# A linear-attention and swish-MoE kernel: how the first two batches load k and v and lead into their first units

## The chip, the cores and the metric

The kernel runs on one core of a Trainium2 chip. Its time is the device time of one execution in microseconds (us); five runs are shown. One more view is the profile of one execution: what each engine did and when. The engines are named as in the profile: PE (TensorE matmul), PEld (its weight loads), DVE (VectorE), ACT (ScalarE), POOL (GpSimd), SP (SyncE, which issues nearly all DMAs).

## The reference

Eight batches, eight heads, 576 tokens, head size 64. Attention is linear: q is normalised by a softmax over its 64 features, k by a softmax over the tokens, and a 64x64 matrix k^T v per head replaces the attention matrix. The result, with heads side by side, goes through two weight matrices with a gated activation between.

```python
q_s = exp(q - max(q));  q_s = q_s / sum(q_s, axis=-1)
k_s = exp(k - max(k));  k_s = k_s / sum(k_s, axis=2)
kv  = einsum('bhsd,bhse->bhde', k_s, v)
att = einsum('bhsd,bhde->bhse', q_s, kv)
x   = att.transpose(0, 2, 1, 3).reshape(4608, 512)
h   = x @ w_in                       # 512 x 2048
g   = h * (1 / (1 + exp(-beta * h)))
out = g @ w_out                      # 2048 x 512
```

## The kernel before

**Tiles.** Each batch gives one chunk of 512 tokens; the last 64 tokens of all eight batches form a ninth chunk. For a chunk, a *unit* is one of 16 column blocks of w_in: `unit_a` (L312) issues four matmuls (K steps, kt = 0 to 3, one per pair of heads) into a PSUM tile `h`, then a tanh on ACT (`th`, L323) and an (th+1)*h on DVE (`g`, L325). `b_mm` (L346) issues the next so many matmuls of the product with w_out, in the order of the list `bq`, each 128x512, into `acc`; at the last of a row block `store` casts to `o` and sends it out.

**Attention of one batch.** `load_q` and `load_kv` fetch 4 heads at a time. k and v have nine tokens per group and a group is spread over two partitions: even partitions take tokens 0 to 4, odd ones tokens 4 to 8, so the fifth token (number 4) is loaded twice. `v_first` (L241) multiplies the first slot by `even`, 1 on even partitions and 0 on odd, so that it counts once; `v_cast` (L250) casts the other four slots of one head to bf16 into `va`. `q_exp`, `q_sum` and `q_div` make the softmax of q, `q_t_pe` (L187) transposes it on PE and copies it out, `k_exp` the exponentials of k. `kv_half` (L258) does for two pairs of heads five matmuls each into one PSUM tile, a reciprocal `rk` and two multiplications into `kvp`. `x_pair` (L282) multiplies a pair's kvp by q^T and casts the result into `xT`, the input of the units.

**What sets the order.** Scheduling is manual: every engine executes in the order in which the code issues. Batch 0's attention stands before all units, with `dummy` matmuls on zeros between (L434 to L474). Batch 1's stands between the units of chunk 0 and those of chunk 1 (L522 to L552), with calls of `b_mm` between its parts: 28, then 8 and 8 around the transposes of q, then three times 4. For later batches the parts hang as hooks on the units of the batch before (L477 to L512). Loads take buffers from one pool `ld` of 13; all of them for the first three batches are issued at the start, on SP's queue: q, k, v of batch 0, w_in, w_out in pairs of blocks, q of batch 1, the rest of w_out, k and v of batch 1, all of batch 2. POOL casts the weights (`cast_w_in`, `cast_w_out`).

**PSUM.** Pools of banks: `psH` 3 (h, and two of chunk 0's acc), `psB` 2 (acc, and the dummies' target), `psX` 2 (x and transposes), `psK` 1 (kv).

Of the kernel before, what the change touches and what calls it, by code (L numbers as in the profile page):

```python
# [9 lines left out]
F32 = mybir.dt.float32  # L10
# [6 lines left out]
def kernel(  # L17
# [61 lines left out]
    def unit(name):  # L79
        return ldp.tile([P, U], F32, tag="ld", name=name)  # L80
# [6 lines left out]
    def load_q(b, hf):  # L87
        t = unit(f"q{b}_{hf}")[:, 0 : 4 * NT * D].rearrange("p (h n) -> p h n", h=4)
        ld["q", b, hf] = t
        nc.sync.dma_start(  # L90
            t,
            q[b, 4 * hf : 4 * hf + 4, 0:CH, :].rearrange("h (p t) d -> p h (t d)", t=NT),
        )
# [6 lines left out]
                t[i * R : (i + 1) * R], q[2 * m + i, :, CH:S, :].rearrange("h s d -> s h d")  # L100
            )

    def load_kv(which, src, b, hf):
        t = unit(f"{which}{b}_{hf}").rearrange("p (h n) -> p h n", h=4)
        ld[which, b, hf] = t
        rows = src[b, 4 * hf : 4 * hf + 4, :, :].rearrange("h (r t) d -> r h (t d)", t=KT9)
        for i in range(2):
            n0 = i * (KT9 - K5) * D
            nc.sync.dma_start(t[i:P:2], rows[:, :, n0 : n0 + K5 * D])

    def load_w_in(n0, n1, k0=0, k1=KT):
        t = unit(f"wi{n0}_{k0}")[:, 0 : (k1 - k0) * (n1 - n0)].rearrange(
# [5 lines left out]
    def load_w_out(j0):  # L118
        t = unit(f"wo{j0}")[:, 0 : 2 * DM].rearrange("p (j n) -> p j n", j=2)
        nc.sync.dma_start(t, w_out_dram[:, j0 : j0 + 2, :])  # L120
        ld["wo", j0] = t
# [4 lines left out]
    def cast(eng, dst, src):  # L126
        if eng is nc.scalar:
            nc.scalar.copy(dst, src)  # L128
        elif eng is nc.gpsimd:
            if len(src.shape) > 3:  # L130
                for i in range(src.shape[1]):
                    cast(eng, dst[:, i], src[:, i])
                return
            n = 1
            for d in src.shape[1:]:
                n *= d
            nc.gpsimd.affine_select(  # L137
                out=dst, in_=src, pattern=[[0, n]], base=0, channel_multiplier=0,
                compare_op=ALU.is_equal, fill=fill0,
            )  # L140
        else:
            eng.tensor_copy(dst, src)  # L142
# [6 lines left out]
    def cast_w_out(j0, eng):  # L149
        cast(eng, w_out_b[:, j0 : j0 + 2, :], ld["wo", j0])  # L150
# [87 lines left out]
            ACTF.Exp,  # L238
        )

    def v_first(b, hf):  # L241
        nc.vector.tensor_scalar(  # L242
            va[b % 2][:, 0, 2 * hf : 2 * hf + 2, 0 : 2 * D].rearrange(
                "p j (two d) -> p j two d", two=2
            ),
            ld["v", b, hf][:, :, 0:D].rearrange("p (j two) d -> p j two d", two=2),
            even[:, 0:1], None, op0=ALU.mult,
        )

    def v_cast(b, h, eng):  # L250
        hf, a = divmod(h, 4)
        cast(
            eng,
            va[b % 2][:, 1:K5, h // 2, (h % 2) * D : (h % 2 + 1) * D],
            ld["v", b, hf][:, a, D:].rearrange("p (t d) -> p t d", t=K5 - 1),
        )

    def kv_half(b, half):  # L258
        ps = psK.tile([P, 2, VW], F32, tag="kv", name=f"kv{b}_{half}")
        for jj in range(2):  # L260
            j = 2 * half + jj
            for t in range(K5):
                nc.tensor.matmul(  # L263
                    ps[:, jj, :],
                    Ek[b][:, t, 2 * j : 2 * j + 2, :].rearrange("p h d -> p (h d)"),
                    va[b % 2][:, t, j, :],
                    start=(t == 0), stop=(t == K5 - 1),
                )
        rk = atn.tile([P, 2], F32, tag="rk", name=f"rk{b}_{half}")
        nc.vector.reciprocal(rk[:], ps[:, :, 2 * D])  # L270
        for h in (0, 1):
            r = slice(h * D, (h + 1) * D)
            nc.vector.tensor_tensor(  # L273
                kvp[b][r, 2 * half : 2 * half + 2, h * D : (h + 1) * D],
                ps[r, :, h * D : (h + 1) * D],
                rk[r, :].unsqueeze(2).to_broadcast((D, 2, D)),
                ALU.mult,
            )

    xT: dict = {}  # L280

    def x_pair(b, j, eng):  # L282
        if b not in xT:
            xT[b] = atn.tile([P, KT, NT, P], BF16, tag="xT", name=f"xT{b}")
        ps = psX.tile([P, NT, P], F32, tag="x", name=f"x{b}_{j}")
        nc.tensor.matmul(  # L286
            ps[:], kvp[b][:, j, :], qT[b][:, :, j, :], start=True, stop=True
        )
        cast(eng, xT[b][:, j], ps[:])

    def x_tail(b, eng):
        ps = psX.tile([P, HP, R], F32, tag="x", name=f"xt{b}")
# [16 lines left out]

    gs: dict = {}  # L310

    def unit_a(n, i):  # L312
        h = psH.tile([P, CH], F32, tag="h", name=f"h{n}_{i}")
        for kt in range(KT):
            nc.tensor.matmul(  # L315
                h[:],
                w_in_b[:, kt, i * P : (i + 1) * P],
                rhs_a(n, kt),
                start=(kt == 0),
                stop=(kt == KT - 1),  # L320
            )
        th = thp.tile([P, CH], BF16, tag="th", name=f"th{n}_{i}")
        nc.scalar.activation(th[:], h[:], ACTF.Tanh, scale=beta_h[:, i : i + 1])  # L323
        g = gtp.tile([P, CH], BF16, tag="g", name=f"g{n}_{i}")
        nc.vector.scalar_tensor_tensor(  # L325
            out=g[:], in0=th[:], scalar=1.0, in1=h[:], op0=ALU.add, op1=ALU.mult
        )
        gs[n, i] = g
        done_a[0] = n * NJ + i
# [53 lines left out]
    for hf in range(2):  # L383
        load_q(0, hf)
    for hf in range(2):
        load_kv("k", k, 0, hf)
    for hf in range(2):
        load_kv("v", v, 0, hf)
    nc.scalar.activation(beta_h[:, 0:1], zero[:, 0:1], ACTF.Exp)
    nc.scalar.dma_start(beta_r[:], moe_beta.rearrange("(j p) -> j p", p=P))  # L390
    load_w_in(0, 256)
# [3 lines left out]
        load_w_in(n0, n0 + 512, 2, 4)  # L395
    for j0 in range(0, 12, 2):
        load_w_out(j0)
    for hf in range(2):
        load_q(1, hf)
    load_w_out(12)  # L400
    load_w_out(14)
    for hf in range(2):
        load_kv("k", k, 1, hf)
        load_kv("v", v, 1, hf)
    for hf in range(2):
        load_q(2, hf)
    for hf in range(2):
        load_kv("k", k, 2, hf)
        load_kv("v", v, 2, hf)

    make_identity(nc, ident[:])
    make_identity(nc, identf[:])
    nc.gpsimd.memset(evens[:], 0.0)
# [16 lines left out]
    def dummy(m, n=CH):  # L430
        for _ in range(m):
            nc.tensor.matmul(warm[:, 0:n], zero[:, 0:P], zero[:, 0:n], start=True, stop=True)  # L432

    dummy(20)  # L434
    q_exp(0, 0, 4)
    q_exp(0, 4, 8)
    q_sum(0, 0, 4)
# [2 lines left out]
    q_div(0, 0, NT, nc.vector, 4, 8)  # L440
    k_exp(0, 0, 4)
    k_exp(0, 4, 8)
    dummy(4)
    for hf in range(2):
        q_t_pe(0, hf, 0, 4, nc.vector)
    bt = psH.tile([P, NJ], F32, tag="h", name="bt")
    nc.tensor.transpose(bt[:], beta_r[:], identf[:])
    nc.vector.tensor_scalar(beta_h[:], bt[:], 0.5, None, op0=ALU.mult)
    def v_casts(b, hf):
        v_first(b, hf)  # L450
        v_cast(b, 4 * hf, nc.gpsimd)
        v_cast(b, 4 * hf + 1, nc.gpsimd)
        v_cast(b, 4 * hf + 2, nc.vector)
        v_cast(b, 4 * hf + 3, nc.scalar)

    v_casts(0, 0)
    dummy(3)
    kv_half(0, 0)
    v_casts(0, 1)
    dummy(4, P)  # L460
    x_pair(0, 0, nc.vector)
    x_pair(0, 1, nc.scalar)
    kv_half(0, 1)
    cast_w_in(0, 0, nc.gpsimd, 0, 128)
    dummy(4, P)
    x_pair(0, 2, nc.vector)
    x_pair(0, 3, nc.scalar)
    cast_w_in(0, 0, nc.gpsimd, 128, 256)
    cast_w_in(256, 0, nc.gpsimd)
    for n0 in (512, 1024, 1536):  # L470
        for k0 in (0, 2):
            cast_w_in(n0, k0, nc.gpsimd)
    for j0 in range(0, 12, 2):
        cast_w_out(j0, nc.gpsimd)  # L474


    hooks: dict = {}  # L477
# [36 lines left out]

    for n in range(NCH):
        for i in range(NJ):
            unit_a(n, i)
            for f in hooks.get((n, i), []):
                f()
            if n:  # L520
                b_mm(2 if n == 1 and i < 4 else 4)
        if n == 0:  # L522
            b_mm(28)
            q_exp(1, 0, 4)
            q_exp(1, 4, 8)
            q_sum(1, 0, 4)
            q_sum(1, 4, 8)
            q_div(1, 0, NT, nc.gpsimd, 0, 4)
            q_div(1, 0, NT, nc.vector, 4, 8)
            cast_w_out(12, nc.scalar)  # L530
            cast_w_out(14, nc.scalar)
            for hf in range(2):
                k_exp(1, 4 * hf, 4 * hf + 4)
            q_t_pe(1, 0, 0, 4, nc.vector)
            b_mm(8)
            q_t_pe(1, 1, 0, 4, nc.vector)
            b_mm(8)
            for hf in range(2):
                v_first(1, hf)
                v_cast(1, 4 * hf, nc.gpsimd)  # L540
                v_cast(1, 4 * hf + 1, nc.gpsimd)
                v_cast(1, 4 * hf + 2, nc.vector)
                v_cast(1, 4 * hf + 3, nc.vector)
            kv_half(1, 0)
            b_mm(4)
            x_pair(1, 0, nc.vector)
            x_pair(1, 1, nc.scalar)
            b_mm(4)
            kv_half(1, 1)
            b_mm(4)  # L550
            x_pair(1, 2, nc.vector)
            x_pair(1, 3, nc.scalar)  # L552
    b_mm(10000)


# [28 lines left out]
```

The softmax here doesn't subtract the row's maximum and nothing guards it: scores larger than these inputs give would overflow.

## Time and profile before

| what | value |
|---|---|
| median of 5 runs | 297.86 us (297.46 to 301.06) |
| time of the run that was profiled | 298.06 us |
| span of the profiled execution | 296.3 us, mean granted clock 0.985 |
| HBM read and written | 38.81 MB and 9.44 MB |
| DMA rate, 8 to 16 us / 18 to 30 us / 40 to 55 us | 355 to 367 / 376 to 390 / 355 to 362 GB/s |
| granted clock, 11.5 to 14.5 us and 42 to 45 us | 0.50 |
| one 128x512 matmul, start to start | about 0.216 us at full clock, 0.43 at half |

How to read it: a row of the timeline gives the start in us, the duration, the engine, the line and operation, output and input tiles with their shapes, and how many were merged; in brackets the idle time before it and what ended that. The chain of waits is followed back from the last instruction: each piece is either work, or the time until what released it. A stretch table gives the busy time of each engine in each stretch. PEclk is the granted TensorE clock, in tenths of full speed.

The main events of the first 65 us, from the timeline: k-v products of batch 0 from 12.61; its first unit from 17.63; w_out products of chunk 0 from 31.52 to 37.87; exponentials of batch 1's q from 35.93 and of its k from 42.03 and 45.65; its k-v products from 46.66 and 51.18; its x pairs from 49.88 and 52.80; its first unit from 53.25.

### The profile page before, as it was taken

What the parts mean: (1) busy time and instruction counts of PE and PEld (TensorE: products, weight loads), DVE (VectorE), ACT (ScalarE), POOL (GpSimd) and SP (SyncE); (2) the same over time, 40 slices, a digit from 0 to 9 for tenths busy, and PEclk for the clock granted to TensorE, in tenths of its full rate; (3) what the DMA queues carried; (4) which work ended last, traced back from release to release, by engine and by line L of the source; (5) the groups of instructions that cost most, each with busy time, mean ns of one, the idle gap of its engine ahead of it and who ended that gap; (6) DMA issues with size and microseconds to landing.
All of it is one profiled execution on the core that took longest, in us unless ns stands there. A gap on an engine that the chain in (4) does not pass through costs nothing.

```text
span 296.3 us, 4129 instructions
## 1 busy us (share of the span) xinstructions
PE 280.7 (95%) x1417; PEld 132.0 (45%) x1444; DVE 165.7 (56%) x307; ACT 168.3 (57%) x268; POOL 73.2 (25%) x121
## 2 busy tenths in 40 slices
PE   8689967999999999999999999999999999999994
PEld 3444434344445444544454444444444444444441
DVE  7868365695686557654665475548544443343300
ACT  4458453683785568646864586458654544454511
POOL 6476631171072006210621063105300000000000
PEclk9799989999999999999999999999999999999998
DMA  7999999719929952997199619931400101031111
GB/s 237 360 383 384 371 365 357 273 56 285 301 82 257 351 76 75 255 354 81 71 228 367 97 73 226 369 63 70 108 18 20 72 36 38 0 71 39 35 71 71
DMA packets 54902, 52.19 MB, mean 176 GB/s; under 512 B 21072, under 2 KB 46688, under 8 KB 54880
## 3 DMA queue, kind: packets, MB, share of 16 engines
q1 hardware_dynamic: 54848, 51.92, 58.4%
q8 instruction: 11, 0.18, 0.3%
q14 instruction: 11, 0.09, 0.1%
q10 hardware_dynamic: 32, 0.01, 0.0%
HBM read 38.81 MB, written 9.44 MB: 163 GB/s over the span
## 4 chain that ended last, share of the span: by engine, by line
PE 78%; DMA 14%; DVE 4%; ACT 1%; issue 1%; POOL 0%; SPq 0%; DVEq 0%; ACTq 0%; POOLq 0%
PE acc L354 38%; PE h L315 35%; DMA wo<-in_moe_w_out_dram 7%; DMA v<-in_v_dram 5%; PE kv L263 3%; PE x L286 2%; DMA q<-in_q_dram 2%; DVE g L325 1%; DVE kvp L273 1%; ACT th L323 1%; DVE xT L142 0%; DVE o L369 0%; DVE qz L173 0%; PE xt L295 0%; DVE va L242 0%
## 5 line engine op out<-in xcount | busy, mean ns | idle before, releaser
L325 DVE SCALAR_TENSOR_TENSOR g<-th,h 128x512 bf16<-128x512 bf16 x144 | 98.6, 685 | 100.9 <-ACT th L323 100.7
L323 ACT ACTIVATE th<-h,beta_h 128x512 bf16<-128x512 f32 x144 | 99.0, 687 | 92.4 <-PE h L315 88.2
L354 PE MATMUL acc<-w_out_b,g 128*128 128x512 bf16 x560 | 145.5, 382 | 0.8
L315 PE MATMUL h<-xT,w_in_b 128*128 128x512 bf16 x502 | 128.2, 379 | 1.1 <-DVE xT L142 0.3
L315 PEld LDWEIGHTS <-w_in_b 128*128 128x128 bf16 x576 | 56.4, 98 | 69.0 <-issue 1.5
L354 PEld LDWEIGHTS <-g 128*128 128x128 bf16 x576 | 55.5, 98 | 64.0 <-issue 2.5
L177 POOL TENSOR_TENSOR Eq<-Eq,qz 128x512 bf16<-128x512 bf16 (+1 forms) x26 | 28.9, 1113 | 97.9 <-DVE qz L174 70.7
L371 ACT ACTIVATE o<-acc 128x512 f32<-128x512 f32 x34 | 20.2, 595 | 9.3 <-PE acc L354 9.3
L235 ACT ACTIVATE Ek<-k 128x640 bf16<-128x640 f32 (+1 forms) x28 | 22.6, 807 | 4.8 <-DMA k<-in_k_dram 4.8
L173 DVE TENSOR_REDUCE qz<-Eq 128x8 f32<-128x512 bf16 (+1 forms) x28 | 21.2, 756 | 3.9 <-ACT Eq L165 3.9
L165 ACT ACTIVATE Eq<-q 128x512 bf16<-128x512 f32 (+1 forms) x28 | 19.3, 690 | 6.8 <-DMA q<-in_q_dram 6.8
L137 POOL TENSOR_SCALAR_AFFINE_SELECT va<-v 128x256 bf16<-128x256 f32 x56 | 20.6, 406 | 9.8 <-DMA v<-in_v_dram 9.8
L315 PE MATMUL h<-xTt,w_in_b 128*128 128x512 bf16 x63 | 16.4, 379 | 0.1
L286 PE MATMUL x<-qT,kvp 128*128 128x512 bf16 x32 | 11.5, 380 | 2.9 <-DVE kvp L273 2.8
L128 ACT CAST xT<-x 128x512 bf16<-128x512 f32 x16 | 9.3, 580 | 7.9 <-PE x L286 7.9
L263 PEld LDWEIGHTS <-Ek 128*128 128x128 bf16 x160 | 10.5, 100 | 6.2 <-issue 4.0
L263 PE MATMUL kv<-va,Ek 128*128 128x130 bf16 x160 | 12.3, 225 | 0.7 <-DVE kvp L273 0.7
L142 DVE CAST xT<-x 128x512 bf16<-128x512 f32 x16 | 11.0, 685 | 1.0 <-PE x L286 1.0
L432 PE MATMUL warm<-zero 128*128 128x512 bf16 (+1 forms) x35 | 9.3, 426 | 1.3 <-DVE zero L382 1.3
L273 DVE TENSOR_TENSOR kvp<-kv,rk 64x128 bf16<-64x128 f32 x32 | 9.2, 289 | 1.3 <-DVE rk L270 0.5
L219 POOL TENSOR_TENSOR Et<-Et,zt 128x512 bf16<-128x512 bf16 x4 | 4.2, 1042 | 22.4 <-ACT th L323 11.4
L137 POOL TENSOR_SCALAR_AFFINE_SELECT w_in_b<-wi 128x1024 bf16<-128x1024 f32 (+1 forms) x9 | 8.5, 945 | 4.3 <-DMA wi<-in_moe_w_in_dram 4.3
(40 smaller groups left out, 70.5 us busy)
## 6 DMA issues: line engine op xcount, KB each, us to landing
k<-in_k_dram SPq DMA_DIRECT2D x32, 320.0 KB, 6.2
v<-in_v_dram SPq DMA_DIRECT2D x32, 320.0 KB, 7.7
q<-in_q_dram SPq DMA_DIRECT2D x16, 512.0 KB, 5.0
out_dram<-o SPq DMA_DIRECT2D x32, 256.0 KB, 2.4
wi<-in_moe_w_in_dram SPq DMA_DIRECT2D x8, 512.0 KB, 9.2
wo<-in_moe_w_out_dram SPq DMA_DIRECT2D x8, 512.0 KB, 12.2
qt<-in_q_dram SPq DMA_DIRECT2D x8, 128.0 KB, 8.4
out_dram<-o SPq DMA_DIRECT2D x8, 128.0 KB, 2.3
```

The source lines that it names most:

```text
L137: nc.gpsimd.affine_select(out=dst, in_=src, pattern=[[0, n]], base=0, channel_multiplier=0, compare_op=ALU.is_equal, fill=fill0,)
L165: nc.scalar.activation(Eq[b][:, :, h0:h1, :].rearrange("p t h d -> p h t d"), ld["q", b, hf][:, a : a + h1 - h0, :].rearrange("p h (t d) - ...
L173: nc.vector.tensor_reduce(qz[b][:, :, h], Eq[b][:, :, h, :], axis=AX.X, op=ALU.add)
L177: eng.tensor_tensor(Eq[b][:, t0:t1, h0:h1], Eq[b][:, t0:t1, h0:h1], qz[b][:, t0:t1, h0:h1].unsqueeze(3).to_broadcast((P, t1 - t0, h1 - h0, ...
L235: nc.scalar.activation(Ek[b][:, :, h0:h1, :].rearrange("p t h d -> p h t d"), ld["k", b, hf][:, a : a + h1 - h0, :].rearrange("p h (t d) - ...
L263: nc.tensor.matmul(ps[:, jj, :], Ek[b][:, t, 2 * j : 2 * j + 2, :].rearrange("p h d -> p (h d)"), va[b % 2][:, t, j, :], start=(t == 0), s ...
L286: nc.tensor.matmul(ps[:], kvp[b][:, j, :], qT[b][:, :, j, :], start=True, stop=True)
L315: nc.tensor.matmul(h[:], w_in_b[:, kt, i * P : (i + 1) * P], rhs_a(n, kt), start=(kt == 0), stop=(kt == KT - 1),)
L323: nc.scalar.activation(th[:], h[:], ACTF.Tanh, scale=beta_h[:, i : i + 1])
L325: nc.vector.scalar_tensor_tensor(out=g[:], in0=th[:], scalar=1.0, in1=h[:], op0=ALU.add, op1=ALU.mult)
L354: nc.tensor.matmul(acc[n, st][:], gs[n, j][:, st * P : (st + 1) * P], w_out_b[:, j, :], start=(j == 0), stop=(j == NJ - 1),)
L371: nc.scalar.activation(o[:], acc[n, st][:], ACTF.Copy, scale=0.5)
```

## The change

In batches 0 and 1 only:

- The fifth token is loaded once: odd partitions take tokens 5 to 8, and their first slot is set to zero by a POOL memset of the tile's first slot (128 x 4 x 64) before the loads. The second v tile of each is loaded in two halves of two heads.
- Batch 1's k is loaded before its v. The loads of batches 1 and 2 are issued in the code after the second cast of w_out on POOL (their place on SP's queue stays).
- `kv_half` is split into `kv_mm` (products of one pair), and `kv_norm` (reciprocal and multiplications of one or two pairs). In `lead_in` pairs 0 and 1 are normalised together, with the lower half on ACT; pairs 2 and 3 one at a time.
- `x_pair` is split into `x_mm` and `x_out`; x of pairs 0 and 1 is cast on ACT, that of pairs 2 and 3 in halves on DVE and ACT. The casts of v are spread in another way over POOL, DVE and ACT.
- `unit_mm` issues a part of a unit's K steps. The first two units of chunk 0, and the first three of chunk 1, have their first three K steps issued right after the last x product; the fourth follows in its old place.
- Batch 0's dummies: 24 instead of 20 and then 4; 3 between the two transposes of q; 4 after them; 2, 3, 2 and 2 wide ones in `lead_in`, where 3 wide and 8 narrow ones stood. Batch 1's calls of `b_mm` in the lead-in keep their sum of 12.

```diff
-    def load_kv(which, src, b, hf):
-        t = unit(f"{which}{b}_{hf}").rearrange("p (h n) -> p h n", h=4)
-        ld[which, b, hf] = t
-        rows = src[b, 4 * hf : 4 * hf + 4, :, :].rearrange("h (r t) d -> r h (t d)", t=KT9)
-        for i in range(2):
-            n0 = i * (KT9 - K5) * D
-            nc.sync.dma_start(t[i:P:2], rows[:, :, n0 : n0 + K5 * D])
+    def load_kv(which, src, b, hf, once=False, h0=0, h1=4):
+        if (which, b, hf) not in ld:
+            t = unit(f"{which}{b}_{hf}").rearrange("p (h n) -> p h n", h=4)
+            ld[which, b, hf] = t
+            if once:
+                nc.gpsimd.memset(t[:, :, 0:D], 0.0)
+        t = ld[which, b, hf][:, h0:h1]
+        rows = src[b, 4 * hf + h0 : 4 * hf + h1, :, :].rearrange("h (r t) d -> r h (t d)", t=KT9)
+        nc.sync.dma_start(t[0:P:2], rows[:, :, 0 : K5 * D])
+        if once:
+            nc.sync.dma_start(t[1:P:2, :, D:], rows[:, :, K5 * D :])
+        else:
+            nc.sync.dma_start(t[1:P:2], rows[:, :, (KT9 - K5) * D :])
...
+    def kv_mm(b, j):
+        if j % 2 == 0:
+            pool, tag = (psB, "acc") if b == 0 and j else (psK, "kv")
+            kvs[b, j // 2] = pool.tile([P, 2, VW], F32, tag=tag, name=f"kv{b}_{j}")
+        for t in range(K5):
+            nc.tensor.matmul(
+                kvs[b, j // 2][:, j % 2, :],
...
+    def kv_norm(b, j, n, eng=None):
+
+        ps = kvs[b, j // 2][:, j % 2 : j % 2 + n, :]
+        rk = atn.tile([P, 2], F32, tag="rk", name=f"rk{b}_{j}")
+        nc.vector.reciprocal(rk[:, 0:n], ps[:, :, 2 * D])
         for h in (0, 1):
             r = slice(h * D, (h + 1) * D)
+            if h and eng is nc.scalar:
+                for m in range(n):
+                    nc.scalar.activation(
+                        kvp[b][r, j + m, h * D : (h + 1) * D], ps[r, m, h * D : (h + 1) * D],
+                        ACTF.Copy, scale=rk[r, m : m + 1],
+                    )
+                continue
...
+    def x_out(b, j, eng, t0=0, t1=NT):
+        cast(eng, xT[b][:, j, t0:t1], xps[b, j][:, t0:t1])
...
+    def unit_mm(n, i, k0, k1):
+        if k0 == 0:
+            hs[n, i] = psH.tile([P, CH], F32, tag="h", name=f"h{n}_{i}")
+        for kt in range(k0, k1):
...
-    dummy(20)
+    dummy(24)
...
-    dummy(4)
-    for hf in range(2):
-        q_t_pe(0, hf, 0, 4, nc.vector)
+    q_t_pe(0, 0, 0, 4, nc.vector)
+    dummy(3)
+    q_t_pe(0, 1, 0, 4, nc.vector)
...
+    dummy(4)
...
+    def lead_in(b, fill):
+        v_first(b, 0)
+        v_cast(b, 0, nc.gpsimd)
+        v_cast(b, 1, nc.gpsimd)
+        v_cast(b, 2, nc.scalar)
+        v_cast(b, 3, nc.scalar if b else nc.vector)
+        fill(0)
+        kv_mm(b, 0)
+        kv_mm(b, 1)
+        v_first(b, 1, 0, 1)
+        v_cast(b, 4, nc.gpsimd)
+        v_cast(b, 5, nc.scalar)
+        kv_norm(b, 0, 2, nc.scalar)
+        if b == 0:
+            kv_mm(b, 2)
+        fill(1)
+        x_mm(b, 0)
+        x_mm(b, 1)
+        v_first(b, 1, 1, 2)
+        v_cast(b, 6, nc.gpsimd)
+        v_cast(b, 7, nc.scalar)
+        if b:
+            fill(2)
+            kv_mm(b, 2)
+        kv_norm(b, 2, 1, nc.vector)
+        x_out(b, 0, nc.scalar)
+        x_out(b, 1, nc.scalar)
+        fill(3)
+        kv_mm(b, 3)
+        x_mm(b, 2)
+        kv_norm(b, 3, 1, nc.vector)
+        x_out(b, 2, nc.vector, 0, 2)
+        x_out(b, 2, nc.scalar, 2, 4)
+        if b == 0:
+            cast_w_in(0, 0, nc.gpsimd, 0, 128)
+            cast_w_in(0, 0, nc.gpsimd, 128, 256)
+        fill(4)
+        x_mm(b, 3)
+        x_out(b, 3, nc.vector, 0, 2)
+        x_out(b, 3, nc.scalar, 2, 4)
+        for i in range(2 + b):
+            unit_mm(b, i, 0, 3)
+
+    def loads_1():
...
+        for hf in range(2):
+            load_kv("k", k, 1, hf, True)
+        load_kv("v", v, 1, 0, True)
+        load_kv("v", v, 1, 1, True, 0, 2)
+        load_kv("v", v, 1, 1, True, 2, 4)
...
+    lead_in(0, lambda m: dummy((2, 3, 2, 2, 2)[m]))
...
     for j0 in range(0, 12, 2):
         cast_w_out(j0, nc.gpsimd)
+        if j0 == 2:
+            loads_1()
...
-            unit_a(n, i)
+            unit_a(n, i, 3 if n < 2 and i < 2 + n else 0)
...
+            lead_in(1, lambda m: b_mm((0, 4, 4, 4, 0)[m]))
```

In batch 0, `lead_in` skips the third fill. Before, batch 1 had this in its place:

```python
            for hf in range(2):
                v_first(1, hf)
                v_cast(1, 4 * hf, nc.gpsimd)
                v_cast(1, 4 * hf + 1, nc.gpsimd)
                v_cast(1, 4 * hf + 2, nc.vector)
                v_cast(1, 4 * hf + 3, nc.vector)
            kv_half(1, 0)
            b_mm(4)
            x_pair(1, 0, nc.vector)
            x_pair(1, 1, nc.scalar)
            b_mm(4)
            kv_half(1, 1)
            b_mm(4)
            x_pair(1, 2, nc.vector)
            x_pair(1, 3, nc.scalar)
```

## The prediction

> **What bounds the kernel now.** I read the page first: shares by engine, the 40 slices, the chain by engine.
>
> ```profile
> span 296.3 us, 4129 instructions
> ...
> PE 280.7 (95%) x1417; PEld 132.0 (45%) x1444; DVE 165.7 (56%) x307; ACT 168.3 (57%) x268; POOL 73.2 (25%) x121
> ...
> PEclk9799989999999999999999999999999999999998
> DMA  7999999719929952997199619931400101031111
> ...
> PE 78%; DMA 14%; DVE 4%; ACT 1%; issue 1%; POOL 0%; SPq 0%; DVEq 0%; ACTq 0%; POOLq 0%
> ```
>
> TensorE is the bound over the whole (95% busy), so what can be won is its idle and half-clock time. The DMA engines are full in slices 1 to 6 and the clock dips in slices 1 and 5: the losses lie before 57 us. From 80 to 280 us a table of stretches gives PE 39.7 to 39.8 of every 40 us: nothing to win there, and the change leaves batches 2 to 7 alone. Next the chain of waits in order of time, from 36 to 56 us:
>
> ```profile
> 31.10 9.03 DMA wo<-in_moe_w_out_dram
> ...
> 40.14 7.22 DMA v<-in_v_dram
> ...
> 47.46 0.57 DVE va L242
> 48.02 0.60 DVE va L142 x2
> 48.62 0.09 DVE rk L270
> ...
> 49.88 0.60 PE x L286 x2
> ...
> 52.81 0.69 DVE o L369
> 53.50 0.61 DVE xT L142
> ...
> 54.16 0.59 PE h L315 x2
> ```
>
> Batch 1's last v tile lands at 47.36; then VectorE casts it (1.2 us) ahead of the reciprocal of the first two pairs, whose products had been ready since 47.39. So 6.8 us pass from landing to the first steady unit at 54.16. The timeline shows the rest:
>
> ```profile
> 2.13 3.79 POOL L426 MEMSET kvp<- 128x512 bf16 x8
> 2.44 3.52 DVE L421 TENSOR_SCALAR va<-va,even 128x8 bf16<-128x8 bf16 x2
> ...
> 40.63 0.62 PE L194 MATMUL tp<-ident,Eq 128*128 128x128 bf16 x8 [2.76 <-POOL Eq L177]
> ...
> 54.78 0.69 ACT L323 ACTIVATE th<-h,beta_h 128x512 bf16<-128x512 f32 x1 [0.75 <-PE h L315]
> ...
> 62.49 1.02 PE L315 MATMUL h<-xT,w_in_b 128*128 128x512 bf16 x4 [0.19 <-DVE g L325]
> ```
>
> PE stands 2.76 us before 40.63, waiting for batch 1's q. So batch 0's lead-in has that slack. At 62.49 PE waits for a g: in stretches of 1 us from 57 to 66, DVE is 0.90 to 1.00 busy. Whatever comes earlier at 54 us must therefore pass through VectorE's queue (g1 at 56.80, then no gap), and that queue starts when ScalarE's th0 does, at 54.78.
>
> **The change, part by part.**
>
> Fewer bytes. The odd partitions' rows of k and v shrink from 1280 to 1024 B in batches 0 and 1: 4 tiles x 256 rows x 256 B = 262 KB a batch. By bytes at the 360 GB/s of that stage: 0.73 us. By packets (the count stays): 2048 B rows moved at about 388 GB/s, 1280 B rows at about 358, or 84.5 and 57.2 ns a packet on each of 16 engines, so 256 B are 9.1 ns; 64 packets an engine: 0.58 us. I take 0.58 a batch. Batch 1's q comes 0.58 earlier, its last v 1.16 (47.36 to 46.2). The order becomes k, k, v, v. From wo's end at 40.1 - 0.58 = 39.5 in tiles of 1.66 us (1.8 less 0.144): k 41.2 and 42.8, first v 44.5, the halves of the second 45.3 and 46.2. Splitting it adds two DMAs a batch on SP's queue; an issue there takes 0.60 us at least, so 1.2 us a batch, before k and q of batch 2. Issue to landing of v was 6.4 us or more, so SP is ahead and I cost it nothing; without that lead 1.2 us.
>
> Eight memsets on POOL. 128x256 f32 has no row; 128x64 f32 took 0.14, 128x128 bf16 0.20, 128x512 bf16 0.52: 0.31 each, 1.24 for four. At the start they precede everything on POOL, so the kvp memsets end at 7.16, not 5.92. The row above shows what that does: two 8-element operations of DVE took 3.4 to 3.5 us and ended at 5.96, with POOL. The Trainium skill, "SBUF — State Buffer", section "Who interferes with whom", says that a VectorE tensor_scalar in a two-port mode and GpSimd share a port pair and the loser blocks for a whole instruction. Read by that, DVE would lose one memset (at most 0.52) and the additions would cost nothing; in the trace it lost all eight. I follow the trace: q_sum and DVE behind it start 1.24 later. The four memsets of batch 1 stand on POOL after w_out's second cast (29.03 + 1.04); SP issued batch 1's first k at 31.73, so they are ready 1 us before, and w_out's casts behind them recover 0.3 us a tile.
>
> Batch 0's lead-in. DVE reached v_first at 11.94, now 13.2. Three wide dummies between the transposes (0.43 each, as the clock is 0.50 from 11.2) put the second transposes at 12.6 to 13.7, its copy to 14.4, v_first to 14.9, the DVE cast to 15.15. Six more dummies end at 15.6, k-v products of two pairs 16.35, reciprocal and normalisation 17.1, then with 7 dummies (0.216 each), two single normalisations and the x pairs, the units start at about 19.7. Before, they ran from 17.7 (31.52 less 64 x 0.216). So 2.0 us later, and 3.5 if the half clock lasts a second 3.4 us. PE then ends its 28 w_out products at 39.9 (or 41.4), where q's transposes are ready at 40.05: the slack is eaten, the loss is small.
>
> The clock in batch 1. It was 0.50 from 41.65 to 45.07. The skill's "TensorE: Matmul & The Clock Gate", section "Why this matters for your kernels", asks for idle gaps of no more than about 3 us; by it neither the 2.76 nor a shorter gap would cost anything. The trace has half clock after 2.76, and after 1.34 followed by transposes (11.2). So a gap may still cost; no gap (39.9 to 40.05) need not. From the first transposes to the k-v products took 6.03 us at the mixed clock; at full clock 0.62 + 1.73 + 0.62 + 1.73 = 4.7. Start S of the products: PE gives 44.8 to 46.1, data 45.35 (v at 44.5, two casts 0.8). I take 45.7; before 46.66.
>
> From S to th0: two products 0.73; reciprocal 0.2; ScalarE's two 64x64 pieces have no row (128x1 ACTIVATE 0.20, 128x256 cast 0.41: 0.27 each) to S+1.5, under four w_out products to 1.6; x0 and x1 2.05; four products 2.9; third pair 3.3 (its half-v and three casts landed long before); four products 4.1; last pair and x2 4.7. On DVE o_3's 0.69 stands ahead of the last reciprocal: 5.0, then 0.17 and two singles of 0.25 to 0.29: x3 at 5.8 to 6.0, nine products of units 0 to 2 by 8.0, hiding x3's half copies (0.4), last K step of unit 0, th0 at S+8.3 = 54.0. Before 54.78.
>
> What is late next: ScalarE and VectorE. th1 no longer waits for PE (th0 to g1 was 2.02, now 0.59 + 0.52 + 0.69 + 0.02 = 1.8): 0.2 more. g4 and the unit at 62.49 come 0.78 + 0.2 = 1.0 us earlier; from there PE is the bound in both. The two more products per unit done ahead gain nothing: they wait there. The other moves (casts from DVE to ACT, x0 and x1 both on ACT, 0.58 each) lie under the w_out products; uncovered 0.6.
>
> Sum: span 296.3 - 1.0 = 295.3. Its run's time was 298.06, 1.76 above span; that gives 297.06, and 0.2 less for the median of 297.86: 296.8.
>
> **The rivals.**
> 1. Larger gain: VectorE is not the limit after 54 us and all of PE's lead counts. PE's effective start was 53.73 (two products done before 54.16) and becomes S+6.05 = 51.4 with S at 45.35: 2.3 us, 295.5. For it: PE 0.81 to 1.00 busy there too. Against: DVE 1.00 in five of those stretches.
> 2. No change: o_3 and the single normalisations stretch the end of batch 1's lead-in by 0.8 us, th0 stays at 54.8: 297.8. For: every step is serial between PE and DVE, as the 1.62 us wait at 49.88. Against: the 1.2 us of v casts ahead of the reciprocal are gone.
> 3. Slower: the half clock. If the thinned work from 11 to 18 us keeps it at 0.50 and batch 0's products slip more than 4.1 us (S past 46.7 moves th0 past 54.98, break-even), each further us counts in full; a second half-clock stretch from 45.07 to 48.5 alone costs 1.7. Together +1.5 to 3.2: 299.4 to 301. For: the dips stand in the trace. Against: after both dips the clock came back in 3.4 us.
> That it doesn't do what it says is excluded: in the program's order the six and nine early K steps stand as described.
>
> **How the numbers follow.** Forecast 57% (gain 0.5 to 1.5), rival 1 13%, rival 2 17%, rival 3 13%. Range 295.2 to 299.2: rival 1 with 0.3 to spare, and the lighter part of rival 3. About 1% (3 us) is what a measurement of this kernel tells from no change: faster by that 7% (half of rival 1, if the lead is larger than worked out), slower 8%, within 85%.
>
> **What would show it.** Right: last v of batch 1 by 46.4; DVE's first 128x8 operations until about 7.2; PE's wait before q's transposes of batch 1 under 1 us; th0 at 53.6 to 54.4; a wait for g at about 61.5. Wrong: last v landing at 47 or later, th0 after 55, PEclk 0.5 after 46 us, or no wait for g near 62.

## The result, and the profile after

| | before | after |
|---|---|---|
| median | 297.89 us (297.36 to 301.06, 44 runs) | 296.31 us (295.98 to 297.43, 23 runs) |
| ratio of after to before, 95% interval | | 0.9932 [0.9915, 0.9949] |
| HBM read | 38.81 MB | 38.28 MB |

The median is 1.58 us (0.5%) lower: inside the 1% that the prediction called "same", at 296.3 us where it had said 296.8, and a little more than the 0.5 to 1.5 us of its forecast. The ratio in the table is that of the means, which lie 2.0 us (0.7%) apart, because 19 of the 44 runs of before took 298.77 us or more. The executions of after fall into two kinds: with the profiled one there are 24, of which 17 have a span of 294.3 to 294.8 us at a granted clock of 0.997 to 1.0, and seven a span of 295.3 to 296.2 (clock 0.994 in six, 0.999 in one). The first profile, of a run of 297.92 us, is the longest of the seven. So it is read here for its mechanisms, and a second profile of the same kernel, from the common kind, for the gain.

First the page of the profiled execution of after; the lines answer to those of before.

```profile
span 296.2 us, 4168 instructions
PE 282.0 (95%) x1421; PEld 131.9 (45%) x1449; DVE 162.5 (55%) x308; ACT 172.1 (58%) x281; POOL 75.3 (25%) x129
PEclk9999989999999999999999999999999999999999
DMA  7999999729929971995199618931500110031111
PE 80%; DMA 11%; DVE 3%; ACT 2%; issue 1%; POOL 1%; SPq 1%; ACTq 0%; POOLq 0%
```

PE is as busy as before. The dip of PEclk in slice 1 (7.4 to 14.8 us) is gone, that in slice 5 (37 to 44.4 us) stands as before. A table of stretches resolves it: a clock of 0.87 from 40 to 42 us, 0.50 from 42 to 44 and 0.78 from 44 to 46. The timeline of the same execution (start, duration, engine, line, operation, tiles, idle time before and what ended it), ordered by stage:

```profile
0.80 0.56 POOL L108 MEMSET k<- 128x256 f32 x2 [0.29 <-POOLq L627]
1.29 0.56 POOL L108 MEMSET v<- 128x256 f32 x2
...
3.42 3.53 DVE L448 TENSOR_SCALAR va<-va,even 128x8 bf16<-128x8 bf16 x2
5.81 1.22 DVE L179 TENSOR_REDUCE qz<-Eq 128x16 f32<-128x1024 bf16 x1
...
12.61 1.16 PE L271 MATMUL kv<-va,Ek 128*128 128x130 bf16 x15
16.86 2.95 PE L350 MATMUL h<-xT,w_in_b 128*128 128x512 bf16 x12
20.22 4.04 PE L350 MATMUL h<-xT,w_in_b 128*128 128x512 bf16 x17 [0.42 <-DVE g L364]
...
24.89 3.33 SPq L90 DMA_DIRECT2D q<-in_q_dram  x2
...
40.55 0.62 PE L200 MATMUL tp<-ident,Eq 128*128 128x128 bf16 x8 [2.76 <-POOL Eq L183]
46.58 0.73 PE L271 MATMUL kv<-va,Ek 128*128 128x130 bf16 x10
...
55.04 0.69 ACT L362 ACTIVATE th<-h,beta_h 128x512 bf16<-128x512 f32 x1 [1.52 <-PE h L350]
...
62.55 1.02 PE L350 MATMUL h<-xT,w_in_b 128*128 128x512 bf16 x4 [0.74 <-DVE g L364]
```

What the reader is to see: the four new memsets shift POOL's start by 0.99 us; the two tiny operations of DVE again last 3.5 us, but the reduction of q (L179) starts at 5.81, as it did before. Batch 0's units start at 16.86 (before: 17.63), but PE then waits, 0.42 us for a g among other things, and w_out products start at 31.44 (before: 31.52). The wait before batch 1's q is 2.76 us, to the digit that of before; k-v products start at 46.58, th0 at 55.04, and the wait for a g at 62.55 lies where it lay before (62.49). In this execution nothing is won.

The second profile, of a run of 296.25 us with span 294.5 and clock 1.00 throughout, shows the kernel as it runs in 17 of 24 executions:

```profile
23.91 3.33 SPq L90 DMA_DIRECT2D q<-in_q_dram  x2
...
34.88 1.06 ACT L171 ACTIVATE Eq<-q 128x1024 bf16<-128x1024 f32 x1 [2.76 <-DMA q<-in_q_dram]
...
39.58 0.62 PE L200 MATMUL tp<-ident,Eq 128*128 128x128 bf16 x8 [2.00 <-POOL Eq L183]
...
44.15 1.24 POOL L143 TENSOR_SCALAR_AFFINE_SELECT va<-v 128x256 bf16<-128x256 f32 x3 [4.62 <-DMA v<-in_v_dram]
...
44.95 0.67 PE L271 MATMUL kv<-va,Ek 128*128 128x130 bf16 x9 [0.79 <-POOL va L143]
46.60 0.61 PE L312 MATMUL x<-qT,kvp 128*128 128x512 bf16 x2
...
50.80 2.52 PE L350 MATMUL h<-xT,w_in_b 128*128 128x512 bf16 x9
...
53.35 0.69 ACT L362 ACTIVATE th<-h,beta_h 128x512 bf16<-128x512 f32 x1 [1.52 <-PE h L350]
...
60.87 1.02 PE L350 MATMUL h<-xT,w_in_b 128*128 128x512 bf16 x4 [0.74 <-DVE g L364]
```

Here SP issues batch 1's q 0.98 us sooner than in the first profile (23.91 against 24.89), everything behind it comes sooner by the same, the clock stays full, and PE has to wait 0.79 us at 44.95 for POOL's casts of the first v: the start of the k-v products (one of them ran ahead at 43.94) is bound by data. th0 comes at 53.35, 1.4 us before that of before (54.78), and the wait for a g ends 1.6 us sooner (60.87 against 62.49). The spans differ by 1.8 us.

### The profile page after: what moved, and what is told of

Its sections match the earlier page's. It is cut to its first block, busy times and chain, and to the rows that moved or that the text cites. A ratio compares the mean times of both kernels' runs of the same rounds, so it can differ in the third digit from the quotient of the medians.

```text
span 296.2 us, 4168 instructions
## 1 busy us (share of the span) xinstructions
PE 282.0 (95%) x1421; PEld 131.9 (45%) x1449; DVE 162.5 (55%) x308; ACT 172.1 (58%) x281; POOL 75.3 (25%) x129
## 3 DMA queue, kind: packets, MB, share of 16 engines
HBM read 38.28 MB, written 9.44 MB: 161 GB/s over the span
## 4 chain that ended last, share of the span: by engine, by line
PE 80%; DMA 11%; DVE 3%; ACT 2%; issue 1%; POOL 1%; SPq 1%; ACTq 0%; POOLq 0%
PE acc L393 39%; PE h L350 36%; DMA q<-in_q_dram 5%; DMA wi<-in_moe_w_in_dram 4%; PE kv L271 3%; PE x L312 2%; DMA v<-in_v_dram 2%; DVE g L364 1%; DVE qz L179 1%; ACT th L362 1%; POOL Eq L183 1%; ACT Eq L171 1%; PE tp L200 0%; DVE kvp L292 0%; SPq L121 0%
## 5 line engine op out<-in xcount | busy, mean ns | idle before, releaser
L179 DVE TENSOR_REDUCE qz<-Eq 128x8 f32<-128x512 bf16 (+1 forms) x28 | 21.2, 756 | 3.9 <-ACT Eq L171 3.9
L134 ACT CAST xT<-x 128x512 bf16<-128x512 f32 (+1 forms) x20 | 10.6, 540 | 2.4 <-DVE xT L148 2.2
L459 PE MATMUL warm<-zero 128*128 128x512 bf16 x39 | 10.7, 420 | 1.3 <-DVE zero L421 1.3
L148 DVE CAST xT<-x 128x512 bf16<-128x512 f32 (+1 forms) x16 | 9.9, 619 | 0.1
L292 DVE TENSOR_TENSOR kvp<-kv,rk 64x128 bf16<-64x128 f32 (+1 forms) x34 | 9.3, 273 | 0.9
```

Of the source, the lines that this page charges most:

```text
L179: nc.vector.tensor_reduce(qz[b][:, :, h], Eq[b][:, :, h, :], axis=AX.X, op=ALU.add)
```

## The experiments

The theory from the first profile of after: the gain is one of data (the first v lands sooner, and the first pairs need no other v), and a stretch of half clock decides in which executions it is had. The rivals: the clock alone (dummy products would do the same for the kernel before), the order alone (without fewer bytes), either batch's part alone. Runs of e and f stand against runs of before on one chip (median of before there 299.2 and 299.1), those of g on another (297.9); ratios are compared, not medians.

### Executions of before

Three more profiles of the kernel before, unchanged; f0 has 12 timed runs too.

> The kernel before, unchanged, for a second profile of it: its runs fall in two groups on one chip, 297.2 to 297.8 and 299.2 to 300.2, at mean clocks that do not tell the groups apart (0.994 is in both), and the changed kernel has no second group. If the second group comes from the half clock falling later in batch 1's lead-in (from 45 us on, behind v's landing), its profile has half clock between 45 and 53 us and q's transposes at 40.6 as before. If it comes from batch 0's lead-in (half clock through the k-v products until 18 us), chunk 0's w_out products end after 40.5 us and q's transposes come later. If from the DMA, v of batch 1 lands 2 us later at an unchanged clock.

> The kernel before, unchanged: another profile, wanted from a run above 299 us. With either lead-in changed alone no run was above 298.8, so the runs above 299 need both old lead-ins. If they are those in which batch 0's half clock lasts to 18 us and delays chunk 0, and a half clock again falls on batch 1's chain behind v, then chunk 0's w_out products end after 40 us and PEclk is 0.5 after 45 us. If the profile is of the lower group: half clock at 11 to 15 and at 41 to 45, th0 near 54.8.

> The same once more: the kernel before, for a profile of a run above 299 us; the same expectations.

Against the other runs of before, f0's gave 1.0006 [0.9981, 1.0031]; its profile (298.24 us) repeats the one shown ahead, with the first x product at 50.03. The runs of before are of two kinds: of the 44, 24 lie at 297.36 to 298.06 and 19 at 298.77 to 301.06, one between. g0 (297.80, span 296.1) and g1 (299.36, span 297.6) are one of each. PE's timeline of g0:

```profile
40.37 1.04 PE L194 MATMUL tp<-ident,Eq 128*128 128x128 bf16 x8 [3.08 <-POOL Eq L177]
41.63 2.48 PE L354 MATMUL acc<-w_out_b,g 128*128 128x512 bf16 x7 [0.22 <-DVE Eq L177]
46.12 0.73 PE L263 MATMUL kv<-va,Ek 128*128 128x130 bf16 x10
49.60 0.60 PE L286 MATMUL x<-qT,kvp 128*128 128x512 bf16 x2 [1.89 <-DVE kvp L273]
52.97 0.59 PE L315 MATMUL h<-xT,w_in_b 128*128 128x512 bf16 x2
```

and of g1, the same kernel:

```profile
40.40 0.62 PE L194 MATMUL tp<-ident,Eq 128*128 128x128 bf16 x8 [3.10 <-POOL Eq L177]
41.08 1.67 PE L354 MATMUL acc<-w_out_b,g 128*128 128x512 bf16 x7
44.76 0.73 PE L263 MATMUL kv<-va,Ek 128*128 128x130 bf16 x10
49.63 1.04 PE L286 MATMUL x<-qT,kvp 128*128 128x512 bf16 x2 [3.28 <-DVE kvp L273]
50.46 1.91 PE L354 MATMUL acc<-w_out_b,g 128*128 128x512 bf16 x4
54.54 0.59 PE L315 MATMUL h<-xT,w_in_b 128*128 128x512 bf16 x2
```

In g0 the half clock falls on the transposes and w_out products at 40 to 44 us (eight transposes 1.04 us, 0.62 at full clock). It costs nothing: the first x product waits for v all the same, and comes at 49.60. In g1 those products run at full clock, PE is through 1.36 us sooner, and then stands 3.28 us; x comes at 49.63, and now the half clock falls on the chain behind it (x 1.04 instead of 0.60, four w_out products 1.91 instead of 1.03), where each lost us counts: units at 54.54 instead of 52.97. The clock averaged over the span is 0.994 in both. So a mean clock doesn't tell what a stretch of half clock costs; its place does. v's landing was the same in both (POOL's last casts began at 47.21 and 47.24). No other run of the upper kind, up to 301.06, has a profile.

### The common execution of after

The kernel after, unchanged; its profile is the second one above.

> The kernel after, unchanged: a look at another execution, since the profiled one was one of the slower seven of its 24 runs. Theory: two things part the executions, when SP can issue batch 1's q (after the landing of w_in's seventh tile) and whether PE's clock stays full from 40 to 46 us. A run of the common group (span 294.3 to 294.8) then has q issued at 23.6 to 24.1, its exponential at 34.6 to 35.0, no half clock from 40 to 46, k-v products waiting for the first v's casts at 44 to 45, and th0 at 53.0 to 53.5. With only one of the two, the span is 295.0 to 295.6; with neither, 296.0 to 296.3. Rival: q's issue is noise that the later stages absorb. Then a run of the common group can have q at 35.5 or later.

The span of 294.5 came with q's issue at 23.91, q's exponential at 34.88, no half clock, th0 at 53.35: all inside the theory's numbers, and the rival (q at 35.5 or later) is out. What ties the issue of q to w_in is in the chain of waits of the first profile (start, duration, what):

```profile
13.64 11.18 DMA wi<-in_moe_w_in_dram
24.83 0.02 SPq L90
24.89 10.94 DMA q<-in_q_dram
```

SP's issue waits for a w_in tile to land, the eighth load before it on that queue. From q's issue everything follows at a fixed distance: the first v's cast on POOL began 20.20 us after it in the first profile and in e3, 20.22 to 20.25 in the second, e1 and f3. So the landing of w_in's seventh tile is what the bytes of batch 0 can move. With the new batch 0 q's issue came at 23.7 to 24.0 in four profiles, at 24.5 in f2's, and at 24.7 and 24.9 in two (mean 24.19). With the old one it came at 24.7 to 25.1 in five. In a sixth, e2's, it came at 24.04 (mean of the six 24.75), but there POOL's cast of the eighth tile began only at 26.02, as late as in the other five (26.05 to 26.48; 25.0 to 25.3 in the four early ones), and the last v was no sooner: POOL cast it from 47.11, against 47.21 in g0.

Late q and half clock came together in the first profile; e3's (below) has them apart. Its kernel differs only behind the last x product, its q was late (24.67) and its clock full, and its k-v products ran on from 45.67. Of the 1.63 us between the two starts, 46.58 and 44.95, q's issue therefore makes 0.98 and the half clock the other 0.65.

### One part undone

Batch 0 as before (loads, dummies, order; batch 1's change stays), then batch 1 as before (k, v, k, v with the fifth token twice, `kv_half`, no early K steps; batch 0's change stays):

```diff
 f1   - load_kv("k", k, 0, hf, True) ... lead_in(0, ...)
      + load_kv("k", k, 0, hf) ... the block of before
      - unit_a(n, i, 3 if n < 2 and i < 2 + n else 0)
      + unit_a(n, i, 3 if n == 1 and i < 3 else 0)
 f2   - load_kv("k", k, 1, hf, True) ... lead_in(1, ...)
      + load_kv("k", k, 1, hf); load_kv("v", v, 1, hf) ... the block of before
      + unit_a(n, i, 3 if n == 0 and i < 2 else 0)
```

> The changed kernel with batch 0 as before (loads with the fifth token twice, v whole, its dummies, its order, no early K steps), batch 1 as changed. Slack theory: batch 0's end has 2.8 us to spare before q of batch 1, so this part is worth nothing by itself: median within 0.4 us of the changed kernel (296.2). Group theory (batch 0's dummies keep the clock up, and that removes the runs at 299 to 300): several of the runs at 298.5 or more, median 0.5 to 2 us above the changed kernel.

> The changed kernel with batch 1 as before (k, v, k, v whole and with the fifth token twice, VectorE's casts ahead of the normalisations, no early K steps), batch 0 as changed. Landing theory: batch 1's lead-in waits for v's landing again, so the gain of the change is gone: lower group at 297.2 to 297.8 as before. If the second group belongs to batch 1's lead-in, it is back (half of the runs above 299); if to batch 0, all runs are below 298.3. Rival (the gain is batch 0's): 296.2.

f1: 297.27 us (296.87 to 298.07, 12 runs), 0.9946 [0.9919, 0.9973]. f2: 297.42 (296.28 to 298.78, 12 runs), 0.9949 [0.9921, 0.9976]. Each part alone has most of the gain, and they don't add up. f1's median is 1 us above that of e1 (below; 296.13 on the same chip), so batch 0's part is worth something, against the theory of slack; and none of its runs is of the upper kind. They win different things. f1 has no run above 298.1, but none below 296.8: its q was issued at 24.87, as in before. f2 has five runs of 296.28 to 296.54, as good as after's common ones, at a clock of 0.997 to 1.0 (none has a profile, so how the old order does as well there stays open), and seven of 297.18 to 298.78 at 0.993 to 0.994. PE's timeline of the profile of one of these:

```profile
44.53 0.73 PE L271 MATMUL kv<-va,Ek 128*128 128x130 bf16 x10
49.01 1.04 PE L312 MATMUL x<-qT,kvp 128*128 128x512 bf16 x2 [2.89 <-DVE kvp L292]
49.84 1.91 PE L393 MATMUL acc<-w_out_b,g 128*128 128x512 bf16 x4
```

That is g1's pattern, 0.6 us earlier: with the old order, where VectorE casts the last v ahead of the first pairs' normalisation, PE stands 2.89 us for it, and the half clock falls behind it. With the new order the first pairs need the first v tile alone, and in its profiles PE waits some 0.8 us at a time, not 3, behind the k-v products.

Third, the fifth token twice in both batches, without memsets; all else as in after:

```diff
-        load_kv("k", k, 0, hf, True)
+        load_kv("k", k, 0, hf)
 (and so in every call that had True)
```

> The changed kernel with the fifth token loaded twice again and no memsets; all else as changed. Data theory (0.58 us a batch by the prediction): v of batch 1 is ready 0.7 to 1.2 us later, and as the k-v products at full clock start when v is cast, th0 is as much later: median 296.9 to 297.4. Rival (PE's order and clock make the gain, data is early enough): 296.1 to 296.5 as the changed kernel.

297.96 us (297.68 to 298.26, 12 runs), 0.9984 [0.9964, 1.0004]: with the bytes put back no gain can be told from zero. That is slower than the 296.9 to 297.4 that was expected. Eight runs had a clock of 0.997 to 0.999 and a span of 295.9 to 296.3, 1.5 to 1.6 us above after's at that clock: the clock alone wins nothing either. The profile has q's issue at 24.70 and the first v's cast 20.68 us behind it, 0.45 more than with one load of the fifth token (the three tiles on the way were worked out at 0.43). With q 0.8 later than in the second profile of after that makes 1.25 of the 1.5 us; the rest stays open. What the order does is seen at the other end: no run above 298.3, where 8 of the 17 runs of before beside it lay above 298.9.

### The split v, and the first wait filled

The second v of batch 1 in two DMAs, not four:

```diff
-        load_kv("v", v, 1, 1, True, 0, 2)
-        load_kv("v", v, 1, 1, True, 2, 4)
+        load_kv("v", v, 1, 1, True)
```

> The changed kernel with batch 1's second v tile loaded by two DMAs again, not four. The DMA rate fell to 217 and 112 GB/s at 43 to 44.5 us in the changed kernel, where four small DMAs stand in SP's queue. If SP's issue of small DMAs makes that hole, it is gone: first v of batch 1 lands at 44.5 and not 45.0, the second by 46.2. At full clock, where the k-v products start when v is cast, 0.3 to 0.5 us faster; at half clock no difference. Rival (the second half's later landing binds the third and fourth pair): slower by 0.3 or more.

296.76 us (296.15 to 297.88, 12 runs), 0.9927 [0.9897, 0.9957], not to be told from after, where 0.3 to 0.5 us faster was expected at full clock. In after's first profile the DMA rate fell to 217 and 112 GB/s in two stretches between 43 and 44.5 us, where SP issued small loads one by one. In e4's it stayed at 347 to 355, but so it did, at 328 to 370, in the second profile of after, where v is split. And from k's first exponential to the first v's cast on POOL it was 3.36 us here (3.33 in after's first profile, hole and all), to POOL's first cast of the last v 5.02 (4.92). So the split alone doesn't make the hole, and in these profiles it costs v nothing.

22 dummy products on zeros before the first transposes of batch 1's q, in after (e1) and in before (e2), to fill the wait for q:

```diff
+            fp = psK.tile([P, 2 * VW], F32, tag="kv", name="fillp")
+            for _ in range(22):
+                nc.tensor.matmul(fp[:], zero[:, 0:P], zero[:, 0 : 2 * VW], start=True, stop=True)
             q_t_pe(1, 0, 0, 4, nc.vector)
```

> The changed kernel with 22 dummy products of 260 columns (0.11 us each, 2.4 us) in PE's wait for batch 1's q. Clock theory: runs of the changed kernel with granted clock 0.994 span 295.3 to 296.2, those with 0.997 to 1.0 span 294.3 to 294.8; the difference is the half clock from 41 to 44.5 us. With the dummies all runs are at full clock and near 294.5 in span, 296.2 in time, none above 296.8; in the profile the k-v products of batch 1 start at 45.8 to 46.0 (bound by the casts of v, which lands at 45.0) and not at 46.58, th0 at 54.2 to 54.4. Data theory (the gain comes from fewer bytes and earlier k and v, the clock only goes along): the same median as the changed kernel within 0.2, with the same spread of 1.5 us.

> The kernel before with the same 22 dummy products in the same wait. Clock theory: before, batch 1's lead-in waits for v's landing at 47.4 and for VectorE's casts behind it, so a full clock only makes PE wait longer at 48 us: time within 0.4 us of the kernel before (297.9). So the change is worth more with the full clock than with the half clock. A plain clock theory (the half clock costs the same in both): 296.5, as fast as the changed kernel. Data theory: no change.

e1: 296.13 us (295.89 to 297.06, 12 runs), 0.9919 [0.9892, 0.9947], and in none of its runs a clock of 0.994 (0.997 to 1.0 in all). Its nine shorter runs are after's common ones; three, of 296.7 to 297.1, are longer at full clock, which fits a late q, though no profile of one was taken; no run above 296.8 had been expected. e2: 299.66 (297.30 to 301.01, 12 runs), 1.0021 [0.9987, 1.0055]: nothing was won. Its profile is of a run of 297.74 us in which chunk 0's w_out products ended only at 40.7, after a half clock that lasted until nearly 22 us. So there the dummies filled no wait; they put the transposes off to 42.99. The clock held full from 40 to 52 us, and the first x product came at 49.51, behind v, as in g0 and g1. Eight of e2's 12 runs lie above 299 us; none of these has a profile. With g2, which at full clock is no faster than the lower kind of before, this puts the rival "the clock alone" out: here the clock is worth something only where PE, and not a landing, sets the end.

### Fewer units ahead

One unit instead of three gets its first three K steps early (e3); and that with e1's dummies (f3):

```diff
-        for i in range(2 + b):
+        for i in range(1 if b else 2):
             unit_mm(b, i, 0, 3)
...
-            unit_a(n, i, 3 if n < 2 and i < 2 + n else 0)
+            unit_a(n, i, 3 if n < 2 and i < 2 - n else 0)
```

> The changed kernel with only one unit of chunk 1 (not three) started three K steps ahead. If VectorE and ScalarE are the limit from th0 to 62 us, the six products of units 1 and 2 that stand before unit 0's last K step only delay th0: th0 comes about 1.0 us after the start of the units, not 2.5, so 1.0 to 1.3 us earlier, limited by x's last copy; the unit that waits for g (62.55) comes 0.6 to 1.2 us earlier: 295.1 to 295.8. Rival (PE is the limit and all early products count): 0.6 to 1.3 us slower, as the six products come later.

> The changed kernel with both: 22 dummies in PE's wait for batch 1's q, and one unit of chunk 1 ahead in place of three. Each took something else away (the half-clock runs at 297; 1 us of th0's delay), so the two add: median 295.0 to 295.4, no run above 296.3. Rival (the dummies only trade the wait): as with one unit ahead alone, 295.6, with its runs at 297.

e3: 295.64 us (295.07 to 297.04, 8 runs), 0.99 [0.9865, 0.9935]. f3: 295.68 (295.14 to 296.22, 6 runs), 0.9904 [0.9875, 0.9933]. f3 was expected at 295.0 to 295.4. The two ratios lie 0.3% under after's, with intervals that overlap its own, so this is a likely gain and not a proven one. e3's timeline shows where it comes from:

```profile
45.67 0.67 PE L271 MATMUL kv<-va,Ek 128*128 128x130 bf16 x9 [0.76 <-POOL va L143]
...
51.52 1.46 PE L350 MATMUL h<-xT,w_in_b 128*128 128x512 bf16 x4
...
53.02 0.69 ACT L362 ACTIVATE th<-h,beta_h 128x512 bf16<-128x512 f32 x1 [0.46 <-PE h L350]
...
60.79 1.02 PE L350 MATMUL h<-xT,w_in_b 128*128 128x512 bf16 x4 [0.25 <-DVE g L364]
```

th0 follows the first early product by 1.50 us; with three units ahead it was 2.55 (50.80 to 53.35), since nine products stand before unit 0's last K step. The lead that PE gains by the early products of the second and third unit is not paid back: ScalarE and VectorE set the pace from th0 on, and the wait for a g shrinks from 0.74 to 0.25 us when they start sooner. In e3's profile q was issued late, at 24.67, and the span is 294.4; in f3's at 23.74, and the span is 293.6. f3's runs lie at 295.14 to 295.28 and 296.08 to 296.22, all at a clock of 0.998 or more. The upper ones have spans of 294.4 to 294.5, as e3's profile with its late q: so the time of q's issue alone is likely worth some 0.9 us.

## Why the prediction was right, step by step

- **Fewer bytes: the mechanism right, one term mis-sized.** The loads shrink as worked out (batch 1's share 0.43 to the first v, measured 0.45). "Batch 1's q comes 0.58 earlier" took the stream of bytes as the limit, and one shift for every execution. q's issue waits for the landing of one w_in tile. On the mean of the profiles it came 0.55 us sooner, about as forecast, but no execution shows that mean: in four of the new batch 0 it was 0.7 to 1.5 us sooner than in before's profiles, in two hardly. In the common kind, that is most of what the gain exceeds the forecast by (span 294.5, where 295.3 was said): v's casts began at 44.15 where its landing was put at 44.5, and the k-v products ran on from 44.95, where the prediction took 45.7 and had 45.35 as its data bound.
- **Memsets: duration right, consequence wrong.** Two take 0.56 us together (0.31 each was said), four shift POOL by 0.99 (1.24 was said). That "q_sum and DVE behind it start 1.24 later" is false: L179 starts at 5.81 in both. The held row's length was read as a delay of the engine. The trace of before had the answer: there too the reduction starts at 5.81, before the held operations' end at 5.96.

```profile
5.81 1.22 DVE L173 TENSOR_REDUCE qz<-Eq 128x16 f32<-128x1024 bf16 x1
```

- **Batch 0's lead-in: wrong, by about 3 us, without effect.** "Units at about 19.7" stood on that delay and on a clock of 0.50 from 11.2. Measured 16.64 to 16.86, at full clock: no profile with the new batch 0 has a dip there, but three of six with the old one have none either, so the dummies get no credit from that. Nor do the runs give it: 7 of f0's 12 and 7 of e2's have a mean clock under 0.99 and none of the 86 with the new batch 0 (g2's among them), but none of f1's 12, with the old one, either. Of the 1.0 us (16.64 against 17.63) 0.3 is left at the w_out products (31.23 against 31.52): PE waits 0.42 for a g and 0.3 for a cast of w_in on the way. And "the slack is eaten" is false: the wait before q stays 1.7 to 2.8 us.
- **The clock in batch 1: seen, its role not.** The prediction let it set the start S and put it in a rival as a second half stretch that makes the kernel slower. In fact it helps to part the executions of both kernels (after's together with q's issue), and what the new order removes is the place where it hurt: the long wait for v, with half clock on the chain behind.
- **From S to th0: right.** 8.3 us was said; measured 8.46 in the first profile (46.58 to 55.04) and 8.40 in the second (44.95 to 53.35). Before it was 8.12 (46.66 to 54.78): the way from S to th0 got 0.3 longer, where rival 2 had 0.8, and what is won is won ahead of S.
- **What is late next: right.** VectorE: 0.90 to 1.00 busy from 57 to 65 us in the first profile, and a wait for g at 60.87 in the second ("about 61.5" was said). e3 shows that the early products of the second and third unit gain nothing there; they likely cost something.
- **Splitting v's load at no cost: right**, as far as e4's runs can tell (to some 0.3%).
- **The number: partly luck.** Of the signs named for "right", the last v came in time in the second profile (POOL's cast at 45.74) and the wait for a g is there (60.87 and 62.55). PE's wait before q's transposes was not under 1 us (2.76 and 2.00), and th0 lay at 53.35 or 55.04, on either side of the 53.6 to 54.4 that was said, in the first profile even beyond the 55 named for "wrong". The loss in batch 0 that was feared did not come, q came earlier in one kind of execution and not in the other, and the upper kind of before, which makes the mean gain 2.0 us, was not in the prediction.
- **Rule against row.** The Trainium skill's "TensorE: Matmul & The Clock Gate", section "Why this matters for your kernels", with its idle gaps of about 3 us, doesn't decide these cases: half clock came after a wait of 1.96 us (g2) and full clock stayed after one of 3.10 (g1). The row was the better guide, but one profile of before showed one of two cases only.

Not settled: why the half clock follows the same wait in one execution and not in the next, and why w_in's seventh tile lands late in some profiles of the new batch 0 and not in others. An execution of after itself with late q and full clock, or early q and half clock, was not profiled; that the runs between 295.3 and 295.7 us of span are these is an inference. f1 and f2 undo several parts at once: batch 0's dummies and the new spread of casts and normalisations were not undone alone.

## What to carry to other kernels

Ask of a stretch of half clock, or of a gap, whether PE or a landing ends last behind it: here it was free before a wait for data (g0) and paid in full behind that wait (g1), and an order that needs only the first tile of a load moves the kernel from the one to the other. Fewer bytes pay where a landing sets the end. The mean rate gave their worth on average (0.58 us worked out, 0.55 measured), but in one execution it was had nearly twice or hardly at all, by the load whose landing releases the next issue. Work pulled ahead should stop at what the next engine can take: with one unit ahead ScalarE started 1.50 us after the first early product, with three 2.55.

## What the hardware showed beyond that

Two 128x8 operations of VectorE beside GpSimd's eight memsets lasted 3.52 us in seven profiles of this case and 0.73 us in the other seven, of the same instructions; in both kinds the next reduction on VectorE started at 5.65 to 5.81. The skill's "SBUF — State Buffer", section "Who interferes with whom", lets the loser block for one instruction: 0.73 fits that (one memset took 0.52), 3.52 doesn't, and neither delayed what came next.
